# Reading the moving operand of two large matrix products as two interleaved halves

## The chip, the cores and the metric

The kernel runs on one core of one Trainium2 chip. The metric is the device time of one execution in microseconds (us); before the change the median of three runs is 882.58 us (882.34 to 883.61). A core has TensorE (PE in the profile, with its weight loads as a row of their own, PEld), VectorE (DVE), ScalarE (ACT), GpSimd (POOL) and SyncE (SP, which here only issues DMAs). They run side by side and meet at semaphores.

## The reference

Linear attention over 8 batches, 8 heads, 576 positions and a head size of 64 is followed by a gated two-layer product over all 4608 tokens, all in float32:

```
q_s = softmax(q, over d)                  # 8 x 8 x 576 x 64
k_s = softmax(k, over the sequence)
kv  = einsum('bhsd,bhse->bhde', k_s, v)
x   = einsum('bhsd,bhde->bhse', q_s, kv)  # as rows: 4608 x 512
h   = x @ w_in                            # 512 -> 2048
g   = h * cos(h)
out = g @ w_out                           # 2048 -> 512
```

The two last products (`x @ w_in` and `g @ w_out`) are the two large ones that the title speaks of.

## The kernel before

**Tiling.** Tokens go in nine blocks of 512: one for each batch (512 of its 576 positions), and a ninth block of what is left over (64 from each of the eight batches), which travels through the DRAM tensor `x_left` and is loaded again by `left()`. The hidden dimension of 2048 goes in 16 chunks of 128. A *unit* is one block with one chunk, 144 in all. `unit1()` makes the 128 x 512 tile `h` (hidden by tokens) with `w_in` as the stationary and `x` as the moving operand; ScalarE and VectorE turn it into `g`; `unit2()` multiplies `g` into the four accumulators `acc` (128 tokens by 512 output columns each), with `g` as the stationary and `w_out` as the moving operand. So `x` moves in the first product (L907) and `w_out` in the second (L987), each time 512 columns of four bytes from one contiguous row of a partition.

**Precision.** A float32 operand is kept as two parts of the type fp32r, a rounded `hi` and the remainder `lo`, and a product is made of three matmuls: hi by hi, hi by lo, lo by hi. With four chunks of 128 rows a unit has 12 matmuls in `unit1` and, with four accumulators, 12 in `unit2`. The first six units differ (`u < F2`): their second product (L980) is made of one plain float32 matmul for each accumulator. That is 144 x 12 + 138 x 12 = 3384 fp32r matmuls of 128 x 512, and 6 x 4 = 24 in plain float32. The attention part makes `x` with matmuls of 288 columns (L767), in plain float32 for the first two batches.

**Weights.** `w_in` and `w_out` come in as 64-bit numbers. `convert()` turns them into float32 (`wc`, or `room` for the first six chunks of `w_out`) and then into hi (ACT, L417) and lo (DVE, L421). For the chunks from 11 on (`FN`) the two weights are converted together in instructions of 1024 elements (`w_io`); the others apart.

**Order.** Nothing is scheduled by hand: every step is given to `Plan` with an engine, an assumed cost, what it reads and writes, and a due time computed from `t0` and `unit`. `plan.order()` simulates the steps as a list scheduler would and emits the instructions of all engines in the order it finds. So a changed cost or due time reorders steps on all engines, DMA issues on SP included. The engines themselves run their queues in that order.

**Rows of the output.** The 512 main positions of a batch are loaded as `(p c)`, so column c*128 + p of `x` is position 4p + c, and accumulator j holds the positions 4p + j; `out_rows()` writes them as rows of 2 KB, four rows apart.

Of the kernel before, what the change touches and what calls it, by code (L numbers as in the profile page):

```python
# [11 lines left out]
F32 = mybir.dt.float32  # L12
# [18 lines left out]
    F2=6,  # L31
# [4 lines left out]


    t0=35.09,
    unit=5.32,
    att0=dict(k=(-5.59, 12.52), kv=(16.57, 0.34), q=(10.64, 24.7), qt=(21.03, 5.77), x=(23.11, -11.12)),  # L40
    att1=(6.26, 6.95),
    att=dict(k=(-1.39, -1.77), kv=(15.07, -0.61), q=(7.54, -0.79), qt=(15.28, 4.51), x=(7.81, 3.15)),
# [150 lines left out]
def linear_attention_then_cos_gated_mlp(  # L193
# [18 lines left out]
    nc = tc.nc  # L212
    B, H, S, D = q.shape
# [124 lines left out]
    def spot(ws, f):  # L338
        return f"w{f}" if f >= FN else f"w{ws}{f}"

    def queue(what, p, seq):

        if seq and (what, p) in CFG["actq"]:
            return nc.scalar, "ACT", [("seq", 1)]
        return nc.sync, "SP", seq
# [26 lines left out]
    def convert(ws, f):  # L372

        n = len(ws)
        R = [("w", w, f) for w in ws]
        wait = ws == "o" and f < F2
        C = room(f) if wait else ring("wc")

        def low():
            return T["raw", ws[0], f][0][:, :, :, 0]  # L380

        def high():
            return T["raw", ws[0], f][0][:, :, :, 1]

        def bias():
            nc.scalar.activation(
                high().bitcast(F32), high().bitcast(F32), AF.Identity, scale=2.0**-112
            )

        def bits():  # L390
            nc.scalar.activation(
                low().bitcast(I32), low(), AF.Identity, bias=0.4996, scale=0.875 * 2.0**-29
            )

        def shift():
            x, y = low().bitcast(I32), high().bitcast(I32)
            nc.vector.scalar_tensor_tensor(
                x, y, 3, x, op0=ALU.logical_shift_left, op1=ALU.bitwise_or
            )

        def sign():
            if wait:
                if ("room", f // 4) not in T:
                    T["room", f // 4] = sbt([P, 4, DM], F32, f"w{NF - 1 - f // 4}", f"room_{f // 4}", 1)
                c = T["wc", ws, f] = T["room", f // 4][:, f % 4 : f % 4 + 1]
            else:
                c = T["wc", ws, f] = sbt([P, 2, DM], F32, "wc", f"wc_{ws}{f}")[:, 0:n]
            nc.vector.scalar_tensor_tensor(
                c.bitcast(I32), high().bitcast(I32), -(2**31), low().bitcast(I32),
                op0=ALU.bitwise_and, op1=ALU.bitwise_or,  # L410
            )

        def hi():
            t = T["wp", ws, f] = sbt([P, n, 2, DM], F32R, spot(ws, f), f"w_{ws}{f}", 1)
            for i, w in enumerate(ws):
                T["w", w, f] = t[:, i]
            nc.scalar.copy(t[:, :, 0], T["wc", ws, f])  # L417

        def lo():
            t = T["wp", ws, f]  # L420
            nc.vector.tensor_sub(t[:, :, 1], T["wc", ws, f], t[:, :, 0].bitcast(F32))  # L421

        act, dve = (0.66, 0.69) if n == 1 else (1.1, 1.22)
        plan.add("ACT", act, bias, writes=R)
        plan.add("ACT", act, bits, writes=R)
        plan.add("DVE", dve, shift, writes=R)
        plan.add("DVE", dve, sign, reads=R, writes=[C])

        def split():
            plan.add("ACT", act - 0.04, hi, reads=[C], writes=R)  # L430
            plan.add("DVE", dve, lo, reads=[C], writes=R)

        if wait:
            splits[f] = split
        else:
            split()


    def load_k(b, p0, np_, tag, due, seq=()):
# [419 lines left out]
    def left(p, due):  # L859
        s, xr = ring("stage"), quarters(ring("x4k"))  # L860

        def load():
            t = T["xlr", p] = sbt([P, TB], F32, "stage", f"xleft_{p}")
            nc.sync.dma_start(t, x_left[p])

        def hi():
            t = T["x", B, p] = sbt([P, 2, TB], F32R, "x4k", f"x_l_{p}")
            nc.scalar.copy(t[:, 0], T["xlr", p])

        def lo():  # L870
            t = T["x", B, p]
            nc.vector.tensor_sub(t[:, 1], T["xlr", p], t[:, 0].bitcast(F32))

        plan.load(0.73, load, reads=[("x_left", p, n) for n in range(B)], writes=[s], due=due)
        plan.add("ACT", 0.62, hi, reads=[s], writes=xr)
        plan.add("DVE", 0.69, lo, reads=[s], writes=xr)
        return xr
# [10 lines left out]
    def unit1(u, xr, due):  # L888
        b, f = order[u][:2]
        h, r = ring("h"), ring("r2")  # L890

        spare = u >= len(order) - 2
        if spare:
            gh = gl = quarters(ring("x4k"))
        else:
            gh, gl = [ring("ghi")], [ring("glo")]

        def g1(chunks):
            if 0 in chunks:
                T["h", u] = bank("h", f"h_{u}")  # L900
            o = T["h", u]
            for c in chunks:
                xh, xl = (T["x", b, c][:, n] for n in range(2))
                cs = slice(c * P, (c + 1) * P)
                wh, wl = (T["w", "i", f][:, n, cs] for n in range(2))
                for n, (a, x) in enumerate(((wh, xh), (wh, xl), (wl, xh))):
                    nc.tensor.matmul(  # L907
                        o, a, x, start=(c == 0 and n == 0), stop=(c == KC - 1 and n == 2)
                    )

        def turns():
            t = T["kt", u] = sbt([P, TB], I32, "r2", f"kt_{u}")
            nc.scalar.activation(t, T["h", u], AF.Identity, bias=0.25, scale=1.0 / TWO_PI)  # L913

        def rest():
            t = T["kt", u]
            nc.vector.scalar_tensor_tensor(  # L917
                t.bitcast(F32), t, -TWO_PI, T["h", u], op0=ALU.mult, op1=ALU.add
            )

        def cos():
            t = T["kt", u].bitcast(F32)
            nc.scalar.activation(t, t, AF.Sin, bias=0.5 * math.pi)  # L923

        def gate():
            t = o = T["kt", u].bitcast(F32)
            if u < F2:
                o = T["g", u] = sbt([P, TB], F32, "ghi", f"g_{u}")
            nc.vector.tensor_mul(o, t, T["h", u])  # L929

        def hi():
            if spare:
                a = sbt([P, 2, TB], F32R, "x4k", f"g_{u}")
                T["gh", u], T["gl", u] = a[:, 0], a[:, 1]
            else:
                T["gh", u] = sbt([P, TB], F32R, "ghi", f"ghi_{u}")
            t = T["gh", u]
            nc.scalar.copy(t, T["kt", u].bitcast(F32))  # L938

        def lo():  # L940
            if not spare:
                T["gl", u] = sbt([P, TB], F32R, "glo", f"glo_{u}")
            t = T["gl", u]
            nc.vector.tensor_sub(t, T["kt", u].bitcast(F32), T["gh", u].bitcast(F32))  # L944

        if u < CFG["early"]:

            for c in range(KC):
                plan.add(
                    "PE", 0.69, lambda c=c: g1([c]), reads=xr[4 * c : 4 * c + 4] + [("w", "i", f)],  # L950
                    writes=[h], due=due,
                )
        else:
            plan.add(
                "PE", 2.73, lambda: g1(range(KC)), reads=xr + [("w", "i", f)],
                writes=[h] + ["last"] * (u == len(order) - 1), due=due,
            )
        plan.add("ACT", 0.6, turns, reads=[h], writes=[r])
        plan.add("DVE", 0.69, rest, reads=[h], writes=[r])
        plan.add("ACT", 0.64, cos, writes=[r], table="sin")  # L960
        if u < F2:
            plan.add("DVE", 0.69, gate, reads=[h, r], writes=gh)
            return gh
        plan.add("DVE", 0.69, gate, reads=[h], writes=[r])
        plan.add("ACT", 0.62, hi, reads=[r], writes=gh)
        plan.add("DVE", 0.69, lo, reads=[r] + gh, writes=gl)
        return gh + gl
# [3 lines left out]
    def unit2(u, g, due, js=range(NJ)):  # L971
# [3 lines left out]
        def g2(j):  # L975
# [9 lines left out]
            wh, wl = (T["w", "o", f][:, n] for n in range(2))  # L985
            for n, (a, w) in enumerate(((gh, wh), (gh, wl), (gl, wh))):
                nc.tensor.matmul(  # L987
                    T["acc", j], a[:, js], w, start=(first and n == 0), stop=(last and n == 2)
                )

        def g2_all():
# [1 line left out]
                g2(j)  # L993

        reads = g + [room(f) if u < F2 else ("w", "o", f)]
        us = 0.86 if u < F2 else 0.683
        if first:
            acc.update({j: ring("acc") for j in range(NJ)})

# [12 lines left out]
    def out_rows(u, j):  # L1012
# [30 lines left out]
        def put():  # L1043
            t = T["o", u, j]
            if cont:
                nc.sync.dma_start(part[b, j], t)
            elif b < B:
                dst = out[b * S : b * S + NM, :].rearrange("(p c) e -> c p e", c=CM)[j]
                nc.sync.dma_start(dst, t)

        if end:
# [160 lines left out]
```

## Time and profile before

| what | us |
|---|---|
| median of three runs | 882.58 |
| span of the profiled execution (first to last instruction) | 878.9 |
| PE busy | 854.4 |
| weight loads on PE (PEld) busy | 697.9 |
| DVE busy | 560.0 |
| ACT busy | 488.5 |
| POOL busy | 31.9 |

The profile is of one execution. Its span leaves out what lies before the first and after the last instruction; the median of the runs is 3.7 us above the span. Matmuls are pipelined: a row's mean duration (390 ns for a 128 x 512 matmul) is longer than the distance to the next one, so that durations can't be added up. In the chain of waits, each piece is charged only with the time until the next piece takes over, and there the distance between two matmuls can be read.

### The profile page before, as it was taken

How to read it: one execution, taken by the hardware profiler on the slowest of the kernel's cores; microseconds unless marked ns; L12 is line 12 of the kernel's file. 1: busy time of each engine (PE TensorE's matmuls, PEld its weight loads, DVE VectorE, ACT ScalarE, POOL GpSimd, SP SyncE). 2: the span in 40 equal slices, each digit the busy share in tenths (PEclk: the TensorE clock that was granted, in tenths of full speed). 3: DMA queues.
4: the chain of work that ended last, by engine and by line, in shares of the span. 5: the costliest groups of instructions: out<-in, count | busy, mean ns of one | idle time of the engine just before them, and what ended most of it. 6: DMA issues, size and time to landing. Idle time of an engine off the chain costs nothing.

```text
span 878.9 us, 11751 instructions
## 1 busy us (share of the span) xinstructions
PE 854.4 (97%) x4308; PEld 697.9 (79%) x4308; DVE 560.0 (64%) x936; ACT 488.5 (56%) x819; POOL 31.9 (4%) x61
## 2 busy tenths in 40 slices
PE   3899999999999999999999999999999999999998
PEld 2656788888888888888888888888888888888886
DVE  7889789987577646764577547764674353333343
ACT  4898888657355636555546545664553353334331
POOL 1200100000000000010000000000000000000000
PEclk9999999999999999999999999999999999999999
DMA  8791465632154204530353034310430020001001
GB/s 236 204 298 38 141 232 175 169 108 74 56 132 109 51 4 123 117 84 3 103 135 84 3 82 129 89 25 31 128 70 16 4 97 1 0 1 49 1 0 49
DMA packets 167226, 75.75 MB, mean 86 GB/s; under 512 B 111360, under 2 KB 157952, under 8 KB 167168
## 3 DMA queue, kind: packets, MB, share of 16 engines
q1 hardware_dynamic: 163904, 72.54, 30.4%
q10 hardware_dynamic: 3264, 2.46, 0.8%
q8 instruction: 34, 0.56, 0.3%
q14 instruction: 24, 0.20, 0.1%
HBM read 55.31 MB, written 19.66 MB: 85 GB/s over the span
## 4 chain that ended last, share of the span: by engine, by line
PE 95%; DVE 2%; DMA 1%; ACT 1%; issue 0%; SPq 0%; DVEq 0%; ACTq 0%
PE h L907 44%; PE acc L987 43%; PE x_False L767 3%; PE acc L980 2%; PE kv L600 2%; DMA q<-in_q_dram 1%; DMA k<-in_k_dram 0%; DVE q L695 0%; DVE qm L676 0%; PE qt L720 0%; DVE k L546 0%; DVE mt L524 0%; DVE qs L687 0%; ACT L683 0%; ACT x L793 0%
## 5 line engine op out<-in xcount | busy, mean ns | idle before, releaser
L907 PE MATMUL h<-x,w_i 128*128 128x512 f32 x1056 | 256.5, 392 | 0.0
L907 PEld LDWEIGHTS h<-x,w_i 128*128 128x128 f32 x1056 | 196.6, 188 | 42.4 <-issue 0.5
L987 PE MATMUL acc<-w_o,ghi 128*128 128x512 f32 x744 | 229.8, 390 | 0.0
L917 DVE SCALAR_TENSOR_TENSOR kt<-kt,h 128x512 f32<-128x512 int32 x144 | 98.7, 685 | 157.5 <-ACT kt L913 157.5
L913 ACT ACTIVATE kt<-h 128x512 int32<-128x512 f32 x144 | 86.0, 597 | 191.5 <-PE h L907 191.3
L987 PEld LDWEIGHTS acc<-w_o,ghi 128*128 128x128 f32 x744 | 139.2, 188 | 28.9
L987 PE MATMUL acc<-w_o,glo 128*128 128x512 f32 x372 | 144.8, 389 | 0.0
L929 DVE TENSOR_TENSOR kt<-kt,h 128x512 f32<-128x512 f32 x138 | 94.4, 684 | 59.7 <-ACT kt L923 58.0
L938 ACT CAST ghi<-kt 128x512 fp32r<-128x512 f32 x136 | 84.2, 619 | 81.1 <-DVE kt L929 70.6
L923 ACT ACTIVATE kt<-kt 128x512 f32<-128x512 f32 x144 | 91.1, 633 | 67.6 <-DVE kt L917 67.3
L944 DVE TENSOR_TENSOR glo<-kt,ghi 128x512 fp32r<-128x512 f32 x136 | 93.6, 688 | 51.0 <-ACT ghi L938 50.8
L907 PE MATMUL h<-x,w_io 128*128 128x512 f32 x480 | 115.4, 389 | 0.0
L987 PE MATMUL acc<-w_io,ghi 128*128 128x512 f32 x344 | 106.3, 390 | 0.0
L907 PEld LDWEIGHTS h<-x,w_io 128*128 128x128 f32 x480 | 89.8, 188 | 18.5
L987 PEld LDWEIGHTS acc<-w_o,glo 128*128 128x128 f32 x372 | 69.8, 188 | 14.6
L987 PEld LDWEIGHTS acc<-w_io,ghi 128*128 128x128 f32 x344 | 63.9, 188 | 12.7
L987 PE MATMUL acc<-w_io,glo 128*128 128x512 f32 x172 | 66.9, 389 | 0.0
L600 PE MATMUL kv<-v_sb,k 128*64 128x66 f32 (+1 forms) x600 | 22.8, 231 | 16.1 <-ACT k L552 16.1
L600 PEld LDWEIGHTS kv<-v_sb,k 128*64 128x64 f32 x600 | 20.0, 143 | 22.8 <-ACT k L552 16.5
L987 PEld LDWEIGHTS acc<-w_io,glo 128*128 128x128 f32 x172 | 32.3, 188 | 6.9
L923 ACT ACT_TABLE_LOAD x27 | 34.6, 1283 | 0.5
L767 PE MATMUL x_False<-qt,kvw 128*128 128x288 f32 x176 | 33.4, 320 | 0.1
(104 smaller groups left out, 747.3 us busy)
## 6 DMA issues: line engine op xcount, KB each, us to landing
out_dram<-o SPq DMA_DIRECT2D x32, 256.0 KB, 2.5
q<-in_q_dram SPq DMA_DIRECT2D x31, 256.0 KB, 3.4
v_sb<-in_v_dram SPq DMA_DIRECT2D x29, 256.0 KB, 3.6
k<-in_k_dram SPq DMA_DIRECT2D x14, 512.0 KB, 4.4
qb<-q_rows SPq DMA_DIRECT2D x96, 72.0 KB, 2.4
q_rows<-q SPq DMA_DIRECT2D x24, 256.0 KB, 2.2
raw_i<-in_moe_w_in_dram SPq DMA_DIRECT2D x10, 512.0 KB, 4.5
raw_o<-in_moe_w_out_dram SPq DMA_DIRECT2D x10, 512.0 KB, 7.1
```

What stands on the lines that cost most here:

```text
L600: nc.tensor.matmul(x[h * D : (h + 1) * D, odd : odd + vt.shape[1]], t[:, h, c, :], vt, start=(c == CM), stop=(c == CM - 1),)
L767: nc.tensor.matmul(t[:, 0:HALF], a, c[:, cs], start=(n == 0), stop=(n == len(parts) - 1 and not again))
L907: nc.tensor.matmul(o, a, x, start=(c == 0 and n == 0), stop=(c == KC - 1 and n == 2))
L913: nc.scalar.activation(t, T["h", u], AF.Identity, bias=0.25, scale=1.0 / TWO_PI)
L917: nc.vector.scalar_tensor_tensor(t.bitcast(F32), t, -TWO_PI, T["h", u], op0=ALU.mult, op1=ALU.add)
L923: nc.scalar.activation(t, t, AF.Sin, bias=0.5 * math.pi)
L929: nc.vector.tensor_mul(o, t, T["h", u])
L938: nc.scalar.copy(t, T["kt", u].bitcast(F32))
L944: nc.vector.tensor_sub(t, T["kt", u].bitcast(F32), T["gh", u].bitcast(F32))
L980: nc.tensor.matmul(T["acc", j], T["g", u][:, js], T["wc", "o", f][:, 0], start=first, stop=last)
L987: nc.tensor.matmul(T["acc", j], a[:, js], w, start=(first and n == 0), stop=(last and n == 2))
```

## The change

In both products the moving operand is read through the view `woven`, `"p (a i) -> p i a"` with a = 2: columns 0, 256, 1, 257, 2, 258 and so on, an element of each half in turn. The result would then come out permuted, so the data is laid out for it. For `w_out` (in `convert`) and the rest block of `x` (in `left`) the hi and lo parts are written with the even elements in the first half and the odd ones in the second (`split` of the target, `dealt` of the source); read back woven, they are in natural order. For the `x` of the eight main blocks nothing is rearranged: the order of the tokens in `h`, `g` and `acc` changes, and the rows to which `out_rows` writes an accumulator change with it (128 rows of 2 KB, now two rows apart within one half of the batch). Where two weights were converted together, hi and lo are now two instructions of 512 elements each in place of one of 1024. The planner's assumed costs of the matmuls and its `unit` are lower, which gives a new order on every engine.

```diff
-    unit=5.32,
+    unit=5.03,
...
+    def woven(t):
+        return t.rearrange("p (a i) -> p i a", a=2)
+
+    def split(t):
+        return t.rearrange("p (a i) -> p a i", a=2)
+
+    def dealt(t):
+        return t.rearrange("p (i a) -> p a i", a=2)
...
-            nc.scalar.copy(t[:, :, 0], T["wc", ws, f])
+            for i, w in enumerate(ws):
+                c = T["wc", ws, f][:, i]
+                if w == "i":
+                    nc.scalar.copy(t[:, i, 0], c)
+                else:
+                    nc.scalar.copy(split(t[:, i, 0]), dealt(c))
...
-            nc.vector.tensor_sub(t[:, :, 1], T["wc", ws, f], t[:, :, 0].bitcast(F32))
+            for i, w in enumerate(ws):
+                c, h, l = T["wc", ws, f][:, i], t[:, i, 0].bitcast(F32), t[:, i, 1]
+                if w == "i":
+                    nc.vector.tensor_sub(l, c, h)
+                else:
+                    nc.vector.tensor_sub(split(l), dealt(c), split(h))
...
-            nc.scalar.copy(t[:, 0], T["xlr", p])
+            nc.scalar.copy(split(t[:, 0]), dealt(T["xlr", p]))
...
-                        o, a, x, start=(c == 0 and n == 0), stop=(c == KC - 1 and n == 2)
+                        o, a, woven(x), start=(c == 0 and n == 0), stop=(c == KC - 1 and n == 2)
...
-                    T["acc", j], a[:, js], w, start=(first and n == 0), stop=(last and n == 2)
+                    T["acc", j], a[:, js], woven(w), start=(first and n == 0), stop=(last and n == 2)
...
-        us = 0.86 if u < F2 else 0.683
+        us = 0.86 if u < F2 else 0.647
...
-                dst = out[b * S : b * S + NM, :].rearrange("(p c) e -> c p e", c=CM)[j]
+                r0 = b * S + j % 2 * (NM // 2)
+                dst = out[r0 : r0 + NM // 2, :].rearrange("(p a) e -> a p e", a=2)[j // 2]
```

Where the two weights of a late chunk are converted together, an instruction is added. These are consecutive rows of DVE at chunk 11 (the lo part `w_io11`, between steps of the units 15 to 17), first before the change and then after it:

```order
L929 TENSOR_TENSOR kt_16_1446<-kt_16_1446,h_16_1410 128x512
L944 TENSOR_TENSOR glo_15_1501<-kt_15_1400,ghi_15_1494 128x512
L421 TENSOR_TENSOR w_io11_1496<-wc_io11_1474,w_io11_1496 128x2x512
L917 SCALAR_TENSOR_TENSOR kt_17_1517<-kt_17_1517,h_17_1476 128x512
L408 SCALAR_TENSOR_TENSOR wc_io12_1523<-raw_io12_1335 128x1024
```

```order
L948 TENSOR_TENSOR kt_16_1528<-kt_16_1528,h_16_1473 128x512
L406 SCALAR_TENSOR_TENSOR raw_io13_1353<-raw_io13_1353 128x1024
L438 TENSOR_TENSOR w_io11_1570<-wc_io11_1553,w_io11_1570 128x512
L440 TENSOR_TENSOR w_io11_1570<-wc_io11_1553,w_io11_1570 128x512
L963 TENSOR_TENSOR glo_16_1608<-kt_16_1528,ghi_16_1603 128x512
L417 SCALAR_TENSOR_TENSOR wc_io12_1613<-raw_io12_1303 128x1024
```

One row of 2 x 512 has become two of 512 (L438 for `w_in`, L440 for `w_out`), and glo of unit 15 now stands ahead of these rows. ACT's hi part is split in the same way; this happens for five chunks.

The start-up is reordered as well. These are rows of PE around the first units, before and after the change (`h_0` and `h_1` are the first product of the units 0 and 1, `kv_1_2` and `kv_1_3` belong to the second batch's attention, `acc_0_0` is unit 0's second product):

```order
L907 MATMUL h_0_439<-x_0_2_469,w_i0_360 128x512 x3
L907 MATMUL h_0_439<-x_0_3_509,w_i0_360 128x512 x3
L907 MATMUL h_1_589<-x_0_0_337,w_i1_511 128x512 x3
L907 MATMUL h_1_589<-x_0_1_368,w_i1_511 128x512 x3
L907 MATMUL h_1_589<-x_0_2_469,w_i1_511 128x512 x3
L907 MATMUL h_1_589<-x_0_3_509,w_i1_511 128x512 x3
L600 MATMUL kv_1_2_616<-v_sb0_87,k_1_2_445 64x66 x2
L600 MATMUL kv_1_2_616<-v_sb0_87,k_1_2_445 64x65 x8
L980 MATMUL acc_0_0_645<-room_0_443,g_0_637 128x512
L600 MATMUL kv_1_3_653<-v_sb1_93,k_1_2_445 64x66 x2
L600 MATMUL kv_1_3_653<-v_sb1_93,k_1_2_445 64x65 x8
```

```order
L619 MATMUL kv_1_2_591<-v_sb0_87,k_1_2_401 64x66 x2
L619 MATMUL kv_1_2_591<-v_sb0_87,k_1_2_401 64x65 x8
L926 MATMUL h_0_445<-x_0_3_548,w_i0_419 128x512 x3
L619 MATMUL kv_1_3_616<-v_sb1_93,k_1_2_401 64x66 x2
L619 MATMUL kv_1_3_616<-v_sb1_93,k_1_2_401 64x65 x8
L926 MATMUL h_1_631<-x_0_0_326,w_i1_536 128x512 x3
L926 MATMUL h_1_631<-x_0_1_405,w_i1_536 128x512 x3
L926 MATMUL h_1_631<-x_0_2_505,w_i1_536 128x512 x3
L926 MATMUL h_1_631<-x_0_3_548,w_i1_536 128x512 x3
L999 MATMUL acc_0_0_666<-room_0_443,g_0_661 128x512
```

The kv products of the second batch have moved ahead of the end of unit 0 and of unit 1; the matmuls themselves are the same in number and shape.

More of the change, by code (lines that the diff above doesn't have):

```diff
@@ L427, in convert, with parts @@
         plan.add("DVE", dve, sign, reads=R, writes=[C])
-        def split():
-            plan.add("ACT", act - 0.04, hi, reads=[C], writes=R)
-            plan.add("DVE", dve, lo, reads=[C], writes=R)
+        def parts():
+            plan.add("ACT", 0.62 * n, hi, reads=[C], writes=R)
+            plan.add("DVE", 0.69 * n, lo, reads=[C], writes=R)
         if wait:
-            splits[f] = split
+            splits[f] = parts
         else:
-            split()
+            parts()
     def load_k(b, p0, np_, tag, due, seq=()):
@@ L867, in hi @@
             t = T["x", B, p] = sbt([P, 2, TB], F32R, "x4k", f"x_l_{p}")
-            nc.scalar.copy(t[:, 0], T["xlr", p])
+            nc.scalar.copy(split(t[:, 0]), dealt(T["xlr", p]))
         def lo():
             t = T["x", B, p]
-            nc.vector.tensor_sub(t[:, 1], T["xlr", p], t[:, 0].bitcast(F32))
+            nc.vector.tensor_sub(split(t[:, 1]), dealt(T["xlr", p]), split(t[:, 0].bitcast(F32)))
         plan.load(0.73, load, reads=[("x_left", p, n) for n in range(B)], writes=[s], due=due)
@@ L949, in unit1 @@
                 plan.add(
-                    "PE", 0.69, lambda c=c: g1([c]), reads=xr[4 * c : 4 * c + 4] + [("w", "i", f)],
+                    "PE", 0.65, lambda c=c: g1([c]), reads=xr[4 * c : 4 * c + 4] + [("w", "i", f)],
                     writes=[h], due=due,
@@ L954, in unit1 @@
             plan.add(
-                "PE", 2.73, lambda: g1(range(KC)), reads=xr + [("w", "i", f)],
+                "PE", 2.59, lambda: g1(range(KC)), reads=xr + [("w", "i", f)],
                 writes=[h] + ["last"] * (u == len(order) - 1), due=due,
```

## The prediction

> **What bounds the kernel now.** I read the page's busy times and slices first, then the chain that ended last, then windows, then the groups of instructions by form.
>
> ```profile
> PE 854.4 (97%) x4308; PEld 697.9 (79%) x4308; DVE 560.0 (64%) x936; ACT 488.5 (56%) x819; POOL 31.9 (4%) x61
> ...
> PE   3899999999999999999999999999999999999998
> ...
> PEclk9999999999999999999999999999999999999999
> ...
> PE 95%; DVE 2%; DMA 1%; ACT 1%; issue 0%; SPq 0%; DVEq 0%; ACTq 0%
> ```
>
> TensorE is busy for 97% of the span at a full granted clock, and 95% of the chain that ended last is TensorE work. Only the first two slices have room. The windows say the same by stretch (columns: length, then busy us and count for PE, PEld, DVE, ACT, POOL):
>
> ```profile
> 0.00:60.00 60.00, 39.77 (x289) 28.73 (x289) 49.72 (x114) 44.57 (x91) 8.77 (x25) 1.00 0.82 234
> 60.00:100.00 40.00, 40.00 (x154) 27.53 (x153) 37.74 (x65) 35.02 (x68) 3.72 (x6) 1.00 0.31 102
> 100.00:200.00 100.00, 100.00 (x511) 82.14 (x510) 85.04 (x130) 73.76 (x115) 2.30 (x4) 1.00 0.57 173
> 640.00:860.00 220.00, 220.00 (x982) 182.58 (x981) 97.66 (x145) 88.70 (x152) 0.00 (x0) 1.00 0.08 22
> ```
>
> From 60 us on PE has no idle time. Up to 100 us VectorE is nearly full too (37.74 of 40 us), then it thins out to 97.66 of 220. So a shorter matmul shortens the span where only PE is full, and little or nothing where others are.
>
> How far apart the matmuls really start is read in the chain (start, us, what), since busy rows overlap:
>
> ```profile
> 59.14 0.44 PE qt L720 x4
> ...
> 62.68 0.97 PE x_False L767 x4
> 63.65 3.43 PE acc L980 x8
> ...
> 118.20 5.44 PE h L907 x24
> ...
> 226.94 0.79 PE x_False L767 x6
> ...
> 863.75 10.89 PE acc L987 x48
> ```
>
> An fp32r matmul of 512 columns takes 5.44/24 = 226.7 ns in the first product and 10.89/48 = 226.9 in the second: one pace, whatever the operand. The plain float32 products stand beside it: 3.43/8 = 428.75 ns. Each of the 24 calls of L980 leaves two such rows, and I read each row as two streams of 512 columns, 214.4 ns a stream. The float32 transposes fit (0.44/4 = 110 ns for twice 128 columns): the line through 256 columns at 110 and 1024 at 428.75 is 0.415 ns a column and 3.8 ns to begin with, which gives 216.3 ns for one stream of 512. So the fp32r matmul is 10.4 to 12.3 ns slower than the array's own pace on the same number of columns, and this is the only thing in the trace that a new order of reading could win.
>
> **The change part by part: the matmuls.** The counts are those of the groups by form:
>
> ```profile
> L907 PE MATMUL h<-x,w_i 128*128 128x512 f32 x1056 | 256.5, 392 | 0.0
> L987 PE MATMUL acc<-w_o,ghi 128*128 128x512 f32 x744 | 229.8, 390 | 0.0
> L987 PE MATMUL acc<-w_o,glo 128*128 128x512 f32 x372 | 144.8, 389 | 0.0
> L907 PE MATMUL h<-x,w_io 128*128 128x512 f32 x480 | 115.4, 389 | 0.0
> L987 PE MATMUL acc<-w_io,ghi 128*128 128x512 f32 x344 | 106.3, 390 | 0.0
> L987 PE MATMUL acc<-w_io,glo 128*128 128x512 f32 x172 | 66.9, 389 | 0.0
> L907 PE MATMUL h<-x_l,w_i 128*128 128x512 f32 x132 | 31.7, 389 | 0.0
> ...
> L907 PE MATMUL h<-x_l,w_io 128*128 128x512 f32 x60 | 14.4, 389 | 0.0
> ...
> L987 PE MATMUL acc<-w_io,g 128*128 128x512 f32 x24 | 5.6, 389 | 0.0
> ```
>
> They add up to 1728 for L907 and 1656 for L987, 3384 in all, the code's number. The float32 matmuls of L980 are not changed.
>
> The trace has no matmul whose moving operand is read in this order, so its cost is bounded from both sides: 214.4 to 216.3 ns if the extra goes, 226.7 if it stays, and 428.75 if every column takes the two steps of a float32 row. I take 216.0, by the nearest rows, those of the same 512 columns without the extra. The reason: in the float32 rows the operand is fetched at half the rate and nothing is added; in the fp32r rows it is fetched at the full rate, one contiguous word after another, and each matmul is late by the same 10.7 ns. Two halves read in turn ask each half for a word only at every second column, the rate that the float32 rows sustain. That is an argument from two rows, not a row that shows it. At 216.0 a matmul gains 226.7 - 216.0 = 10.7 ns.
>
> Not every one lies where PE sets the pace. The same windows for L907 alone and for L987 alone:
>
> ```profile
> 0.00:60.00 60.00, 13.06 (x50) 9.02 (x50) 1.00 0.82 234
> 60.00:100.00 40.00, 17.93 (x72) 12.99 (x70) 1.00 0.31 102
> 100.00:200.00 100.00, 51.53 (x216) 40.53 (x217) 1.00 0.57 173
> ```
>
> ```profile
> 60.00:100.00 40.00, 5.25 (x21) 4.10 (x22) 1.00 0.31 102
> 100.00:200.00 100.00, 49.59 (x203) 37.20 (x201) 1.00 0.57 173
> ```
>
> 50 matmuls stand before 60 us, where loads, DVE and ACT set the pace: nothing gained. 93 stand between 60 and 100: 93 x 10.7 ns = 1.0 us, of which I count half, as DVE is at 94% there. 3241 come after: 34.7 us. Together 35.2 us.
>
> [...]
>
> **The conversions.** The rows of ACT and DVE that they concern:
>
> ```profile
> L386 ACT ACTIVATE raw_i<-raw_i 128x512 f32<-128x512 f32 x11 | 7.5, 682 | 1.5 <-DMA raw_i<-in_moe_w_in_dram 1.5
> ...
> L417 ACT CAST w_io<-wc_io 128x1024 fp32r<-128x1024 f32 x5 | 5.3, 1051 | 0.9 <-DVE wc_io L408 0.9
> ...
> L417 ACT CAST w_o<-wc_o 128x512 fp32r<-128x512 f32 x5 | 3.1, 619 | 0.0
> ```
>
> ```profile
> L408 DVE SCALAR_TENSOR_TENSOR wc_i<-raw_i 128x512 int32<-128x512 int32 x11 | 7.5, 685 | 0.1
> ...
> L421 DVE TENSOR_TENSOR w_io<-wc_io,w_io 128x1024 fp32r<-128x1024 f32 x5 | 6.1, 1212 | 0.2 <-ACT w_io L417 0.2
> ...
> L421 DVE TENSOR_TENSOR w_o<-wc_o,w_o 128x512 fp32r<-128x512 f32 x5 | 3.4, 684 | 0.4 <-ACT w_o L417 0.4
> ```
>
> Five pairs become two instructions each: ACT 5 x (2 x 619 - 1051) = 0.9 us more, DVE 5 x (2 x 684 - 1212) = 0.8 us. The sources are now read two words apart, in 16 + 4 instructions on each engine. On DVE, L408 already reads its raw words so and takes 685 ns, as contiguous L421 does: nothing. On ACT the nearest strided row, L386, has 682 ns against 619; at worst 20 x 63 ns = 1.3 us. All of this stands beside PE: the weights are converted before 200 us, mostly in the window from 100 to 200 in which PE is full and DVE has 15 us, ACT 26 us to spare; the four of the rest block come after 640 us, where both are half idle. I count nothing; without that cover it would cost 0.8 us on DVE or 2.2 on ACT.
>
> **Rows of the output and the new order.** As many DMAs of as many 2 KB rows are issued on SP, to other rows, and nothing waits for them but a buffer. The order changes everywhere. From 60 us on PE is full and its list of work is the same, so an exchange of rows there costs nothing as long as an operand doesn't come late; that cover is thinnest up to 200 us. In the start-up, PE waits 20.2 of 60 us, and the order sets for what. The largest waits there that an exchange can remove or add once are of this kind:
>
> ```profile
> 40.69 2.77 DMA q<-in_q_dram
> ...
> 46.71 0.73 PE kv L600 x20
> ```
>
> The moved kv products are 0.73 us a pair; the load that the second batch's queries wait for is 2.77. I take 0 for the start-up and keep 2.8 us on both sides. The tail after the last matmul stays.
>
> **The sum.** 878.9 - 34.7 - 0.5 = 843.7 us of span. The median lies 3.7 us above the span; with it the time is **847.4 us**.
>
> **The rivals.**
>
> *The extra stays (no change).* If the 10.7 ns belong to each matmul rather than to the reading, weaving does nothing. For it: the fp32r matmuls of 288 columns take 0.79/6 = 131.7 ns, and half a float32 row of the same width is 0.97/8 = 121.3, so 10.4 ns are added there too, nearly as many as for 512 columns. Against it: a weight load goes with each of them and is long beside so short a stream, which may account for that one:
>
> ```profile
> L767 PEld LDWEIGHTS x_False<-qt,kvw 128*128 128x128 f32 x176 | 28.0, 191 | 4.6 <-issue 1.3
> ...
> L980 PEld LDWEIGHTS acc<-room,g 128*128 128x128 f32 x48 | 8.8, 190 | 10.8 <-issue 8.1 <-DVE g L929 2.3
> ```
>
> 191 ns of load against 121 ns of stream, where 226.7 covers it; and the float32 rows have a load for each row as well, without the extra. Then the time is 882.6 us, give or take the 2.8 us of the start-up.
>
> *Reading in jumps is slower (the other side).* Woven, no column follows its predecessor in memory. If such a column can't be fetched within one step of the array, each takes two, as in a float32 row: 428.75 - 226.7 = 202 ns more for 3384 matmuls, 684 us, a time of 1566 us. It decides early: a matmul loses as soon as more than (226.7 - 216.0)/0.415 = 26 of its 512 columns wait one step longer. For it: no row of the trace reads a moving operand in jumps; against it: DVE reads words two apart at full pace (685 ns), though at a slower step. [...]
>
> *The others become the bound.* If DVE and ACT hold PE up to 200 us, the 93 matmuls and the 216 + 203 of the next window gain nothing: 35.2 - 0.5 - 4.5 = 30.2 us gained, 852.4 us. For it: DVE at 94% and 85%. Against: after the gain of 4.5 us DVE would be at 85.9 of 95.5 us, still under PE.
>
> **How the numbers follow.** The extra goes: 0.78. The others become the bound: 0.04. It stays: 0.10. Slower reading: 0.08. The first case by itself reaches from 882.6 - 3384 x 12.3 ns - 2.8 = 838 to 882.6 - 3241 x 10.4 ns + 2.8 + 2.2 = 854 us, which holds the second too: 0.82, so the range is 838 to 854. A measurement of this kernel can tell about 0.2% (1.8 us) from no change. Of the case in which the extra stays I give 0.02 to faster, 0.05 to the same and 0.03 to slower, by the new order. Faster 0.78 + 0.04 + 0.02 = 0.84, same 0.05, slower 0.03 + 0.08 = 0.11.
>
> **What would show it.** In the chain of the changed kernel, runs of 24 or 48 matmuls of both products should stand at 216 ns each, those of L980 unchanged at 429 a row. The split casts should show about 619 and 684 ns each. If the pace is 226.7, the extra belongs to something else; if only one product is faster, it hangs on the operand. PE must stay full from 60 to 860 us (now less), and the windows to 200 us show whether DVE or ACT now make it wait. Wrong would be above all the step from the float32 rows to the woven ones.

## The result and the profile after

The changed kernel takes 851.2 us (median of 4 runs, 850.55 to 852.07) against 883.1 us before on the same chip (4 runs, 882.34 to 884.25): a ratio of 0.9643, with a 95% interval of 0.9629 to 0.9658, or 31.9 us less. That is inside the range of 838 to 854 us, and 3.8 us above the forecast of 847.4.

First the page of the changed kernel: busy times, and the shares of the chain that ended last.

```profile
PE 819.0 (97%) x4308; PEld 702.4 (83%) x4308; DVE 569.7 (67%) x941; ACT 498.4 (59%) x824; POOL 30.2 (4%) x61
...
PE 86%; ACT 6%; DVE 3%; DMA 2%; SPq 2%; issue 2%; POOL 0%; ACTq 0%; DVEq 0%
```

PE's busy time has fallen by 35.4 us (854.4 to 819.0), the span only by 30.3 (878.9 to 848.6). DVE and ACT have become busier, each by 10 us (560.0 to 569.7, 488.5 to 498.4), and a chain that was 95% PE is now 86% PE, with ACT and DVE in it. The chain in order of time gives the pace (start, us, what):

```profile
58.76 3.43 PE acc L999 x8
...
166.62 5.18 PE h L926 x24
...
830.99 12.96 PE acc L1006 x60
```

5.18/24 = 215.8 ns in the first product and 12.96/60 = 216.0 in the second, where 226.7 and 226.9 stood; the float32 rows are unchanged (3.43/8 = 429 ns). The pace is what was forecast. The windows show where the rest went (columns: length, then busy us and count for PE, PEld, DVE, ACT, POOL):

```profile
0.00:60.00 60.00, 38.35 (x285) 28.35 (x286) 50.16 (x114) 44.51 (x91) 9.01 (x25) 1.00 0.86 252
60.00:100.00 40.00, 40.00 (x171) 27.65 (x170) 38.59 (x62) 37.74 (x68) 3.72 (x6) 1.00 0.24 76
100.00:200.00 100.00, 96.76 (x497) 82.84 (x496) 92.70 (x136) 80.94 (x118) 0.64 (x3) 1.00 0.58 173
200.00:640.00 440.00, 440.00 (x2410) 384.98 (x2409) 298.67 (x498) 254.98 (x413) 16.88 (x28) 1.00 0.32 81
```

Between 100 and 200 us PE, which had no idle time before, is now idle for 3.2 us, beside a DVE that is busy for 92.7 us instead of 85.0 and an ACT with 80.9 instead of 73.8. PE's waits from 60 to 200 us name the releasers (us in total, times, longest):

```profile
PE h L926 <- DVE kt L948: 2.4, 3, 1.2
PE acc L1006 <- DVE glo L963: 0.5, 1, 0.5
PE acc L1006 <- ACT o L1055: 0.3, 1, 0.3
```

The PE counts of the windows say where the gain lies. Before the change 954 matmul rows stand ahead of 200 us (289 + 154 + 511), after it 953 (285 + 171 + 497): up to there nothing was gained, and the 30.3 us of the span were all won behind it.

The groups by form say why DVE and ACT are late. These are rows of the weight conversion, first before the change and then after it. All of these instructions read or write words two apart, but for L417 (before) and L429 (after), which are one and the same cast:

```profile
L397 DVE SCALAR_TENSOR_TENSOR raw_i<-raw_i 128x512 int32<-128x512 int32 x11 | 7.7, 696 | 0.6 <-ACT raw_i L391 0.6
...
L391 ACT ACTIVATE raw_i<-raw_i 128x512 int32<-128x512 uint32 x11 | 7.4, 672 | 0.0
...
L417 ACT CAST w_i<-wc_i 128x512 fp32r<-128x512 f32 x11 | 6.8, 617 | 0.4 <-DVE wc_i L408 0.4
...
L397 DVE SCALAR_TENSOR_TENSOR raw_io<-raw_io 128x1024 int32<-128x1024 int32 x5 | 6.1, 1221 | 0.0
```

```profile
L400 ACT ACTIVATE raw_i<-raw_i 128x512 int32<-128x512 uint32 x11 | 8.9, 811 | 0.0
...
L429 ACT CAST w_i<-wc_i 128x512 fp32r<-128x512 f32 x11 | 6.8, 615 | 1.0 <-DVE wc_i L417 1.0
...
L431 ACT CAST w_o<-wc_o 128x512 fp32r<-128x512 f32 x5 | 4.2, 842 | 0.0
...
L406 DVE SCALAR_TENSOR_TENSOR raw_i<-raw_i 128x512 int32<-128x512 int32 x11 | 8.9, 808 | 0.4 <-ACT raw_i L400 0.2
L406 DVE SCALAR_TENSOR_TENSOR raw_o<-raw_o 128x512 int32<-128x512 int32 x11 | 8.7, 799 | 0.8 <-ACT raw_o L400 0.8
L406 DVE SCALAR_TENSOR_TENSOR raw_io<-raw_io 128x1024 int32<-128x1024 int32 x5 | 8.6, 1718 | 0.5 <-ACT raw_io L400 0.5
...
L440 DVE TENSOR_TENSOR w_o<-wc_o,w_o 128x512 fp32r<-128x512 f32 x5 | 4.1, 826 | 0.1
```

L400 and L406 (L391 and L397 before) are instructions that the change does not touch: 672 ns before and 811 now on ACT, 696 and 808 on DVE, 1221 and 1718 for the long ones. The means of the short ones mix stages: from 100 to 200 us alone, where the long ones stand too, `raw_o` takes 928 ns on ACT instead of 668 and 932 on DVE instead of 684. L429, which reads contiguous words, has kept its duration (617 ns before, 615 now). So the PE's new way of reading seems to slow what ACT and DVE do with a step of two words; and the order of the start-up is new. Two theories for the missing time stand beside each other: **contention** and **order**.

### The profile page after: what moved, and what is told of

It reads as the page before. It is cut to its first block, busy times and chain, and to the rows that moved or that the text cites. A ratio compares the mean times of both kernels' runs of the same rounds, so it can differ in the third digit from the quotient of the medians.

```text
span 848.6 us, 11759 instructions
## 1 busy us (share of the span) xinstructions
PE 819.0 (97%) x4308; PEld 702.4 (83%) x4308; DVE 569.7 (67%) x941; ACT 498.4 (59%) x824; POOL 30.2 (4%) x61
## 4 chain that ended last, share of the span: by engine, by line
PE 86%; ACT 6%; DVE 3%; DMA 2%; SPq 2%; issue 2%; POOL 0%; ACTq 0%; DVEq 0%
PE h L926 39%; PE acc L1006 39%; PE x_False L786 3%; PE acc L999 2%; PE kv L619 2%; DMA part<-o 1%; DMA k<-in_k_dram 1%; ACT k L571 1%; ACT L942 0%; ACT kt L932 0%; SPq L827 0%; ACT kt L942 0%; ACT raw_i L400 0%; ACT raw_io L395 0%; DVE q L698 0%
## 5 line engine op out<-in xcount | busy, mean ns | idle before, releaser
L926 PE MATMUL h<-x,w_i 128*128 128x512 f32 x1056 | 244.5, 382 | 1.8 <-DVE kt L948 1.8
L1006 PE MATMUL acc<-w_o,ghi 128*128 128x512 f32 x744 | 221.6, 379 | 0.3 <-ACT o L1055 0.3
L1006 PE MATMUL acc<-w_o,glo 128*128 128x512 f32 x372 | 141.2, 380 | 0.5 <-DVE glo L963 0.5
L926 PE MATMUL h<-x,w_io 128*128 128x512 f32 x480 | 110.1, 379 | 0.6 <-DVE kt L948 0.6
L1006 PE MATMUL acc<-w_io,ghi 128*128 128x512 f32 x344 | 102.9, 381 | 0.0
L1006 PE MATMUL acc<-w_io,glo 128*128 128x512 f32 x172 | 65.2, 379 | 0.0
L786 PE MATMUL x_False<-qt,kvw 128*128 128x288 f32 x176 | 35.2, 324 | 1.3 <-ACT qt L769 0.8
```

The source lines that it names most:

```text
L786: nc.tensor.matmul(t[:, 0:HALF], a, c[:, cs], start=(n == 0), stop=(n == len(parts) - 1 and not again))
L926: nc.tensor.matmul(o, a, woven(x), start=(c == 0 and n == 0), stop=(c == KC - 1 and n == 2))
L1006: nc.tensor.matmul(T["acc", j], a[:, js], woven(w), start=(first and n == 0), stop=(last and n == 2))
```

## The experiments

**Order and reading taken apart.** The first kernel is the changed one with the planner's old numbers, so that all engines run in the order of before but for the split casts; the second is the kernel of before with the new numbers. Two of these numbers are shown; the assumed costs of `unit1()` and of the hi and lo parts change with them.

```diff
 # e1: changed kernel          # e2: kernel of before
-    unit=5.03,                 -    unit=5.32,
+    unit=5.32,                 +    unit=5.03,
...
-        us = 0.86 if u < F2 else 0.647
+        us = 0.86 if u < F2 else 0.683
```

> The changed kernel with the planner's old costs and unit, so that every engine's order is that of before (but for the split casts). Theory one, contention: the woven reading slows the strided instructions of ACT and DVE (in the changed kernel 676 to 812 ns and 691 to 803 ns for the same instruction), and those 10 us per engine are what PE waits for; then the old order gives the same slow conversions and a time of 850 to 853 us. Theory two, the order: the new order of the start-up and up to 200 us costs the missing 6 us; then this kernel takes 845 to 847 us. In both, a matmul of 512 columns stands at 216 ns.

> The kernel of before, contiguous reading, with the new planner costs, so that every engine's order is that of the changed kernel (but for the split casts). Theory one, contention: conversions stay at 676 and 691 ns as before, and the time is that of before, 882 to 884 us. Theory two, the order: 4 to 6 us are lost, 887 to 889 us. In both, matmuls stand at 227 ns.

e1 took 848.28 us, a ratio of 0.9616 (0.9599 to 0.9633); e2 884.29 us, 1.0023 (1.0011 to 1.0036). Both lie between the theories' numbers, so that each is right in part. The new order costs 2.0 us on contiguous reading (1.0 to 3.2 by the interval), and 2.4 us would be its price on woven reading (0.9643 against 0.9616), but there the intervals overlap a little, so that this alone would not show it. But the order of before does not bring all of it back. The window from 100 to 200 us, first of e1 and then of e2, and a conversion on ACT in each:

```profile
100.00:200.00 100.00, 97.82 (x518) 83.81 (x517) 93.94 (x138) 83.53 (x123) 3.68 (x6) 1.00 0.57 173
```

```profile
L400 ACT ACTIVATE raw_o<-raw_o 128x512 int32<-128x512 uint32 x11 | 8.6, 790 | 0.0
```

```profile
100.00:200.00 100.00, 99.45 (x504) 81.50 (x499) 84.58 (x129) 72.69 (x113) 0.61 (x2) 1.00 0.57 170
```

```profile
L391 ACT ACTIVATE raw_o<-raw_o 128x512 int32<-128x512 uint32 x11 | 7.4, 687 | 0.0
```

Woven reading in the order of before leaves PE idle for 2.2 us and the conversion at 790 ns; with contiguous reading it stays at 687, though in the new order. The slow conversions follow the reading, not the order.

**Is it the step of two words?** In e5 the conversion takes contiguous halves of the raw words (and masks that keep the numbers finite, one of them read as an integer): not the reference's weights, but the same instructions in the same order.

```diff
-            return T["raw", ws[0], f][0][:, :, :, 0]
+            return T["raw", ws[0], f][0].rearrange("p n e t -> p n (e t)")[:, :, 0:DM]
...
-        return t.rearrange("p (i a) -> p a i", a=2)
+        return split(t)
```

> The kernel of e1_woven_old_order (woven reading, order of before) in which the conversion's instructions read and write contiguous words: the raw words are taken as two contiguous halves instead of every second word, and the parts of w_out are made without the rearrangement, with bit masks that keep the numbers finite. So the weights are not those of the reference; what is left out is the right choice of words. Count, order and sizes of all instructions stay. If the woven reading slows only strided accesses of ACT and DVE, all conversions return to 620 to 690 ns, PE's waits between 100 and 200 us (2.2 us in e1) fall to under 1 us, and the time is 845 to 847 us. If it is rather the faster PE that shortens every deadline, the waits stay at about 2 us and the time at 848 us.

844.36 us, a ratio of 0.9571 (0.9557 to 0.9586), clear of e1's interval; by the ratios that is 4.0 us less than e1. Its conversions and its window:

```profile
L400 ACT ACTIVATE raw_o<-raw_o 128x512 int32<-128x512 uint32 x11 | 6.8, 627 | 0.0
L431 ACT CAST w_o<-wc_o 128x512 fp32r<-128x512 f32 x5 | 3.1, 620 | 0.3 <-DVE wc_o L417 0.2
```

```profile
100.00:200.00 100.00, 100.00 (x533) 86.88 (x533) 89.32 (x142) 75.53 (x124) 2.29 (x4) 1.00 0.60 178
```

PE is full again at the faster pace. So ACT and DVE have enough time here for a PE at 216 ns a matmul (busy for 75.53 and 89.32 of the 100 us), and it is the slowing of strided accesses that they lack time for. One reserve is left: contiguous conversions on ACT are also a little shorter here than the strided ones were before the change (626 ns for `raw_i` instead of 672). A run below (e11) settles it.

**A planner that knows it.** e6 is e1 with the measured durations given to the planner (one of three changed lines is shown; the others set the hi and lo parts).

```diff
-        act, dve = (0.66, 0.69) if n == 1 else (1.1, 1.22)
+        act, dve = (0.8, 0.8) if n == 1 else (1.55, 1.67)
```

> e1_woven_old_order with the planner told what the conversions took there (0.8 us in place of 0.66 on ACT and 0.69 on DVE, 0.85 and 0.84 for the parts of w_out). If PE's waits up to 200 us come from an order that was planned with conversions that are too short, they fall and the time is 846 to 847.5 us; if ACT and DVE simply lack the time there, it stays at 848 us within 1.

Neither: 856.14 us, 0.9699 (0.968 to 0.9719), slower than e1 by 7.3 us. In its trace PE is busy for 36.92 of the first 60 us and for 95.28 of the 100 from 100 us on. Truer costs gave a worse order here, in the start-up too. Why was not followed up; it is one kernel, and it says only that a truer cost need not bring a better order of this list scheduler.

**Which readings have the pace of 216 ns?** My reason was that each half is asked for a word only at every second column. The next kernels are that of before in its own order; only the address order of the moving operand differs, so that the output comes out permuted.

```diff
-                        o, a, x, start=(c == 0 and n == 0), stop=(c == KC - 1 and n == 2)
+                        o, a, seen1(x), start=(c == 0 and n == 0), stop=(c == KC - 1 and n == 2)
...
+        return t.rearrange("p (a i b) -> p i a b", a=2, b=2)   # e3, first product; b=4 second, b=16 e4
+        return t.rearrange("p (i a) -> p a i", a=2)            # e4, second product
+        return t.rearrange("p (a i) -> p i a", a=4)            # e7, first product
+        return t.rearrange("p (o a i) -> p o i a", a=2, i=4)   # e7, second; i=2 and i=32 e8
```

> The kernel of before in its order; only the address order of the moving operand is changed, with no layout to match, so that h's columns and the output's columns come out permuted. First product: two contiguous columns of each half in turn; second product: four of each half in turn. If the extra of 10.7 ns goes wherever two distant places are read in turn, both stand at 216 ns. If only a column that does not directly follow its neighbour in memory is free of it, the first stands at about 221 and the second at about 224 ns. If each jump costs something by itself, the first is slower than the second. For the conversions: if jumps are what slows them, they lie between 676 and 812 ns on ACT.

> As the run before it, output permuted. First product: sixteen columns of each half in turn; second product: the even columns, then the odd ones (a step of two words, no second half). If reading two distant places in turn is what helps, the first stands at 216 and the second at 227 ns. If any step other than one word helps, the first stands near 226 and the second at 216 ns. If bandwidth in bytes sets the pace, both stand at 227; if a step over a word costs a fetch, the second is slower than 227 ns.

> The kernel of before in its order, only the address order of the moving operand changed, output permuted. First product: one column of each of four quarters in turn; second product: halves of four columns in turn (0, 4, 1, 5 and so on), two places 16 bytes apart. If one word of each place in turn is what helps, wherever the places are, both stand at 216 ns. If it needs two far places, the second stands at 227 ns or above. If four places are too many, the first is over 227 ns.

> As the run before it. First product: 0, 2, 1, 3 and so on, within four neighbouring words; second product: halves of 32 columns in turn, 128 bytes apart. If any swap of the order of words helps, the first stands at 216 ns; if a place must be left for another one at each column, the first is at 227 ns or above and the second at 216 ns; if the distance must be more than 128 bytes, neither is at 216 ns.

The chain's rows, of e3, e4, e7 and e8 in turn:

```profile
236.87 8.02 PE h L913 x24
...
1086.43 12.01 PE acc L993 x48
```

```profile
253.60 5.76 PE h L913 x24
...
1250.63 21.76 PE acc L993 x48
```

```profile
448.17 6.76 PE h L913 x24
...
936.59 10.37 PE acc L993 x48
```

```profile
412.46 5.48 PE h L913 x24
...
851.09 10.37 PE acc L993 x48
```

| order of the columns | ns a matmul |
|---|---|
| contiguous (before) | 226.7 |
| one word of two places in turn, 4 words apart (e7) | 10.37/48 = 216 |
| the same, 32 words apart (e8) | 10.37/48 = 216 |
| the same, 256 words apart (the change) | 216 |
| 0, 2, 1, 3 within four words (e8) | 5.48/24 = 228 |
| one word of four places in turn (e7) | 6.76/24 = 282 |
| two words of two places in turn (e3) | 8.02/24 = 334 |
| four words of two places (e3) | 12.01/48 = 250 |
| sixteen words of two places (e4) | 5.76/24 = 240 |
| every second word (e4) | 21.76/48 = 453 |

Of the orders tried, only one form has 216 ns: a single word of each of two places, four or more words apart. Two distant places in turn are not enough (334, 250, 240), leaving the contiguous order is not enough (453, 228), and four places are worse than one (282 against 226.7). My reason would have put pairs and fours at 216 too; it falls. Why this one form is fast stays open. The whole runs, one of each, took 1104 (e3), 1278 (e4), 953 (e7) and 867 us (e8). The conversions that stride are as before in e4, although its first product reads two places 1 KB apart (677 to 684 ns on ACT, 671 to 682 before; the long one on DVE 1224, before 1221), and in e8, with its 216 ns in the second product, too (679 to 686; 1230): the distance, or how often the places alternate, or the pace, must matter to them. What the conversions took in e3 and e7 is not shown.

**Nearer places, as a whole kernel.** e7 and e8 have the pace with places 16 and 128 bytes apart. The next two are whole kernels in the order of before, with x woven 128 columns apart and w_out 32, laid out to match; they differ in how the output's rows come out right.

```diff
+    NX, NW = 128, 32
-        return t.rearrange("p (a i) -> p i a", a=2)
+        return t.rearrange("p (o a i) -> p o i a", a=2, i=n)
...
+                for i in range(2):                       # the first: two DMAs
+                    nc.sync.dma_start(dst[i], t[i::2])
...
-            js = slice(j * P, (j + 1) * P)               # the second: stationary operand with a step of two
+            js = slice(j // 2 * 2 * P + j % 2, (j // 2 + 1) * 2 * P, 2) if b < B else slice(j * P, (j + 1) * P)
```

> The order and planner costs of before, with the two places nearer: x read in halves of 128 columns within 256 (512 bytes apart), w_out in halves of 32 within 64 (128 bytes apart), laid out to match; an accumulator's rows go out in two DMAs of every second partition. If the slow conversions come from places 1 KB apart, they are back at 676 to 690 ns (850 for none), all matmuls stand at 216 ns, PE's waits between 100 and 200 us are under 1 us, and the time is 844 to 846 us. If any weaving of x slows them, they stay above 780 ns and the time is 848 us.

> As the run before it, but each accumulator takes every second column of g as its stationary operand, so that the rows of the output are those of before, in one DMA. If a weight load with a step of two words stays hidden under a 216 ns matmul, the time is that of the run before it within 1 us. If it costs what a moving operand with a step of two costs (452 against 227 ns in e4), the second product's pace becomes that of its weight loads, near 300 ns or more, and the time is over 950 us.

845.93 us, 0.9589 (0.9569 to 0.9608), and 844.62 us, 0.9569 (0.9553 to 0.9585): both intervals lie clear of the changed kernel's, the second's also of e1's. The second's window, a conversion, and its weight loads:

```profile
100.00:200.00 100.00, 100.00 (x533) 88.21 (x532) 93.16 (x142) 80.76 (x125) 2.48 (x5) 1.00 0.60 179
```

```profile
L402 ACT ACTIVATE raw_o<-raw_o 128x512 int32<-128x512 uint32 x11 | 8.2, 758 | 0.0
...
L1008 PEld LDWEIGHTS acc<-w_o,ghi 128*128 128x128 f32 x744 | 144.5, 195 | 16.2
```

PE is full, though the conversions are only partly faster (758 ns where e1 had 790; the long one on DVE 1487 where e1 had 1675). In the first of the two they are no better (ACT 753 to 804 ns, where 676 to 690 were expected with a time of 844 to 846): its time came as expected and the reason for it did not. How much of the gain over e1 comes from the long conversions was not taken apart. A weight load with a step of two takes 195 ns, where the first kernel's has 189, and the second product keeps 10.37/48 = 216 ns with it.

**Distance or operand?** Again the kernel of before with another address order alone: both products woven 32 words apart, or only x, 256 words apart.

```diff
+        return t.rearrange("p (o a i) -> p o i a", a=2, i=32)    # e11, both products
+        return t.rearrange("p (o a i) -> p o i a", a=2, i=256)   # e12, first product alone
```

> The kernel of before in its order, only the address order of the moving operand changed, output permuted. Both products read halves of 32 columns in turn, 128 bytes apart. Both stand at 216 ns. If the distance of the two places decides whether strided conversions are slowed, they take 676 to 690 ns as in e8 and the time is about 844 us, since the conversions are those of before; if it is the weaving of x at any distance, ACT takes about 770 and DVE about 800 ns as in e9, and the time is 845 to 847 us.

> As the run before it, but only the first product is read woven, in halves of 256 columns, 1 KB apart; the second reads contiguous words. The first stands at 216 ns, the second at 227. With 1728 matmuls faster by 10.7 ns, 18.5 us at most, the time is 864 to 867 us. If weaving x is what slows the conversions, they stay near 800 ns; if both products share in it, they lie between 690 and 780 ns; if it was the woven w_out, they are at 676 to 690 ns.

e11 took 843.56 us, 0.9564 (0.9539 to 0.9589); e12 867.43 us, 0.9833 (0.9808 to 0.9858), just above the 864 to 867 expected. The pace of both products, and a conversion on ACT and one on DVE, of e11 and then of e12; between them e11's window:

```profile
116.96 5.18 PE h L913 x24
...
827.32 10.37 PE acc L993 x48
```

```profile
L397 ACT ACTIVATE raw_o<-raw_o 128x512 int32<-128x512 uint32 x11 | 7.4, 686 | 0.0
...
L403 DVE SCALAR_TENSOR_TENSOR raw_o<-raw_o 128x512 int32<-128x512 int32 x11 | 7.5, 693 | 0.0
```

```profile
100.00:200.00 100.00, 100.00 (x534) 86.88 (x533) 89.33 (x136) 76.96 (x120) 2.30 (x4) 1.00 0.60 179
```

```profile
121.03 5.18 PE h L913 x24
...
852.06 10.92 PE acc L993 x48
```

```profile
L397 ACT ACTIVATE raw_o<-raw_o 128x512 int32<-128x512 uint32 x11 | 7.9, 727 | 0.0
...
L403 DVE SCALAR_TENSOR_TENSOR raw_o<-raw_o 128x512 int32<-128x512 int32 x11 | 8.4, 771 | 0.0
```

With places 128 bytes apart both products have the pace and the conversions nearly the durations of before (686 and 693 ns; 679 and 685 before); with places 1 KB apart even one product slows them (727 and 771). So at the pace of 216 ns the distance decides in these kernels: 1 KB, and 512 bytes for x (the two whole kernels above, 755 and 758 ns for the same row of ACT), slow them, 128 bytes does not, and what lies between was not tried. Distance alone does not: e4 takes sixteen words of each of two places 1 KB apart at a slower pace (240 ns), and does not slow the conversions (681 ns for that row). The mechanism was not settled.

e11 also settles what e5 left open. Its conversions stride as before and take nearly what they took before (686 ns for `raw_o` on ACT instead of 679), its PE is as fast as the changed kernel's (216 ns in both products), and PE is full from 100 to 200 us. In the order of before, 977 matmul rows stand ahead of 200 us in e11 (287 + 156 + 534), 953 in e1 (279 + 156 + 518) and 954 before the change. By e11, contention costs e1 4.6 us (0.9616 against 0.9564), the split casts included.

## Why the prediction was right, and where it was wrong

- **The pace**, the step on which most of it hung, was right to 0.2 ns: 216.0 forecast, 215.8 and 216.0 measured in the two products. With 3384 matmuls the most it can give is 3384 x 10.9 ns = 36.9 us.
- **The reason given for it was wrong.** "Two halves read in turn ask each half for a word only at every second column" would have made pairs and fours as fast. The runs show a single word of each of two places as the only form of those tried. The bounds from the float32 rows (214.4 to 216.3 ns) were right where the reason was not, so that it was luck that the change has the one form that reaches the lower bound.
- **The extra stays** fell: the same weight loads go with each matmul in the changed kernel (189 ns a load, 188 before) and in e11 (533 loads beside 534 matmul rows from 100 to 200 us), at 216 ns a matmul. The extra of 10.4 ns at 288 columns, which spoke for it, is no sign of a fixed price of a matmul then; whether the weight loads account for it there was not tried.
- **Slower reading** fell for this order and was right for another. Every second word takes 453 ns, twice the contiguous 226.7, about what the rival priced for jumps (428.75). Why leaving the neighbour costs nothing in the one order and doubles the time in the other, no run shows.
- **The conversions** are the step that failed: both their cost and the cover for it. I took "nothing" on DVE and at worst 63 ns an instruction on ACT from rows of before, in which PE read contiguously. Measured: 826 to 909 ns for L440 where 684 was taken, 790 to 914 for L431 where 619 was, and more on instructions that the change does not touch. In place of 0.8 and 0.9 us (2.2 with the stride's worst), DVE and ACT have 10 us more each, most of it before 200 us. The cover that I named, 15 us of DVE and 26 of ACT between 100 and 200, was there on average, and yet PE waited 3.2 us. e1 against e5 prices this at 4.0 us, e1 against e11 at 4.6.
- **The others become the bound** came true in its time: nothing was gained up to 200 us (953 matmul rows against 954), and its 852.4 us lie nearer to the measured 851.2 than my 847.4. It came by another mechanism than the faster PE alone, which e5 and e11 exclude, since PE is full in both: the slower conversions, with a part for the order. I had given it 0.04.
- **The new order**, taken as 0 with 2.8 us on both sides, costs 2.0 to 2.4 us (e2, and e1 against the changed kernel). The start-up shows part of it: PE is busy for 38.35 of the first 60 us, against 39.77.
- **The sum.** With the order of before and no contention, e11 takes 0.9564 of 882.04 us, a gain of 38.5 us, which is the 36.9 within its interval of 2.2 us. From it go 4.0 to 4.6 for contention and 2.4 for the order: 31.5 to 32.1, against 31.9 measured. Both deductions are differences between runs that lead from e11 or e5 to the changed kernel, so the sum has to close as nearly as e5 and e11 agree (0.9571 and 0.9564); it is a summary and no further test. I had 35.2: the pace's 36.2 (at 10.7 ns) less 1.0 us for matmuls off the path, and nothing for the other two. The range held the time because its upper end allowed 2.8 us for the order and 2.2 for the conversions; the order stayed under the first, and contention took about twice the second.

## What to carry to other kernels

Here a moving fp32r operand read as one word of each of two places in turn brought a matmul from 226.7 to 216 ns, and the places may be near: four words apart have the same pace as 256 (216 ns), and 128 bytes apart left the other engines' durations nearly as they were (686 ns instead of 679 for `raw_o` on ACT). When one engine's accesses change, the durations of instructions that nobody edited need not be those of the old trace (672 to 811 ns on ACT); where one has little time to spare, as DVE between 100 and 200 us (85.0 us busy before the change), 112 to 260 ns more for a conversion of 512 elements came back with 3.2 us of waits on PE. And when a change also reorders a whole program, run the old order with the new work and the new order with the old work: each took one kernel here. They showed that there were two causes; the price of the first took a third kernel that has the pace without the contention (e5, e11).

## What the runs showed of the hardware that I had not expected

- The moving operand's pace depends on the form of its address order between 216 and 453 ns for the same 512 columns, as the table above has it. Every second word takes as long as two contiguous readings (453 ns against 226.7, e4); pairs taken alternately (334 ns) are slower than fours (250, both e3).
- PE's alternate reading of words 1 KB apart slowed reads and writes of ACT and DVE that have a step of two words, by 12 to 41% between 100 and 200 us (668 to 928 and 1133 to 1500 ns on ACT, 684 to 932, 1221 to 1718 and, for `wc_o`, the least, 689 to 775 on DVE), and left contiguous ones nearly as they were (617 and 615 ns on ACT for `w_i`, L417, now L429; 685 and 702 on DVE for `w_i`, L421, now L438, which takes 742 for `w_io`). Words 128 bytes apart left the short strided ones on ACT at 684 to 695 ns in e11, against 671 to 682 before.
- A weight load of 128 columns with a step of two words takes 195 ns instead of 189 (the second of the two whole kernels), where a moving operand with the same step takes twice its time (453 ns against 226.7, e4).
